# A planner's attention figures and its idle products, in a fused RWKV-5 and tanh-shrink kernel

## The chip, the cores and the metric

The kernel runs on one core of one Trainium2 chip. The metric is the device time of one execution in microseconds; shown is the median of three runs. TensorE is called PE below, VectorE DVE, ScalarE ACT, GpSimd POOL, and SyncE SP.

## The reference

Two stages follow each other. The first is a linear attention with a decaying state per head; the second is a two-layer block with the activation h - tanh(h). Cut to what matters:

```python
B, H, S, D = 4, 8, 768, 48
for t in range(S):
    cur = einsum('bhd,bhe->bhde', u * k[t], v[t])
    y[t] = einsum('bhd,bhde->bhe', r[t], state + cur)
    state = w * state + einsum('bhd,bhe->bhde', k[t], v[t])
x = y.transpose(0, 2, 1, 3).reshape(B * S, H * D)      # 3072 tokens x 384
h = x @ w_in                                           # 384 -> 2048
out = (h - tanh(h)) @ w_out                            # 2048 -> 384
```

## The kernel before

**Attention.** The sequence is cut into chunks of 64 steps. A unit is one chunk of two batch rows, so there are 24 units; unit n has the half n % 2 of the batch rows and the chunk n // 2. Its work runs through four engines in this order. SP loads r, k and v (`rt`, `kt`, `vt`; L750, three units' buffers each). DVE scales k for the state (`kw`, L894). PE turns r and `kw` with the identity into PSUM ("turn", eight products each, L763). ACT copies the turned k (`kT`, L776) and DVE scales the turned r (`rT`, L767). PE multiplies the state by `rT` ("from_state", 16 products) and `kT` by `rT` ("levels", 16 products). DVE has formed r times k and its sum (`rk` L780 and L909, `du` L784), from which ACT writes the diagonals (`at`, L788); DVE then copies the masked levels over them (`at`, L919). PE multiplies `at` by v ("outputs") and v by `kw` (the new state). ACT copies the outputs out (`xt` and `rest`, L855), DVE adds the state (L882) and decays it (L928), and POOL moves the part called `rest` into place with six small DMAs (L876). All of this PE work has the line of one helper (L717) in the profile, apart from the turns. The PSUM tile `yk_ps` holds both outputs and new state, so from_state of the next unit waits until ACT and DVE have emptied it.

**Dense part.** Two units, or 256 tokens, make one of the 12 groups j. A hidden tile is one group and two blocks of 128 hidden columns: six products h (L168, two halves of three), five ACT steps (`s`, `th`, `tg`, `q`, `small`), four DVE steps (`g` L192, `c1` L194, `c2` L196, and the masked copy over `g` at L198), and four products o (L206). Later tiles take seven half-width products of sums in place of eight (L257), for which POOL forms the sums (L242 to L246) and DVE the mixed weights (L266). The weights come as 64-bit words and are converted by DVE and ACT (L137 to L143) in 16 pieces. Passes over the first six groups take 4, 4 and 8 of the 16 hidden blocks, so that a pass needs only the pieces that are already converted.

**Order.** Nothing of this order is written by hand. Each step is a task with an engine, a cost in us, its predecessors, and a number of PE instructions (`steps`). The planner `Plan` runs forward through the tasks as the engines would, picks on each engine the ready task that is due first, and searches at random from a fixed seed for due times that end earlier. The program is then written engine by engine in that order, so any figure of a cost can move tasks on every engine. The planner also follows PE's instruction fetch: each 256 steps it works out when the next block has come, and makes PE wait if that is late.

**Idle products.** Up to the first o, the planner puts products of the identity with itself (L655) into the gaps of its plan on PE. They write a PSUM tile that nobody reads. A wide one has 512 columns and the planner's cost 0.9, a narrow one 256 columns and 0.46. `filled` counts how many fit between PE's last task and the next one:

```python
        for cost, run in filling[2]:
            n = max(0, int((start - free) / (cost * (2 if start < self.WARM else 1))))
            free += n * cost
            runs += [run] * n
        return runs
```

Of the kernel before, what the change touches and what calls it, by code (L numbers as in the profile page):

```python
# [300 lines left out]
class Plan:  # L301
# [15 lines left out]
    def add(self, engine, cost, run, after=(), due=1e9, data=0, gated=False, steps=0):  # L317
        t = SimpleNamespace(engine=engine, cost=cost, run=run, after=[x for x in after if x], due=due, data=data,
                            gated=gated, steps=steps, then=[], n=len(self.tasks))
        for x in t.after:  # L320
            x.then.append(t)
        self.tasks.append(t)
        return t
# [12 lines left out]
    def forward(self, due, until=1e9):  # L336

        ready = [max(self.FIRST, due[t.n] - self.EARLY) if t.gated else 0.0 for t in self.tasks]
        count = [len(t.after) for t in self.tasks]
        waiting = self.queues(ready, count)  # L340
        free, lanes, channel = dict(self.BEGIN), {}, 0.0
        step, bound, comes, fills = 0, self.CHUNK_0, 0.0, iter(self.fills)
        filling = next(fills, None)
        starts, done, last, first, changed = [None] * len(ready), [], 0.0, {}, set(waiting)
        self.fitted, work = [], {}
        while len(done) < len(ready):
            for e in changed:
                ts = waiting[e]
                first.pop(e, None)
                if not ts:  # L350
                    continue
                start = max(free.get(e, 0.0), min(ready[x.n] for x in ts))
                t = min((x for x in ts if ready[x.n] <= start + 1e-9), key=lambda x: (due[x.n], x.n))
                if t.data:
                    start = max(start, lanes.setdefault(e, [0.0] * self.LANES)[0])
                else:

                    soon = [x for x in ts if ready[x.n] < start + t.cost and due[x.n] < due[t.n] - self.SPARE]
                    if soon:
                        t = min(soon, key=lambda x: (ready[x.n], x.n))  # L360
                        start = max(start, ready[t.n])
                first[e] = start, t
            e = min(first, key=lambda x: (first[x][0], x))
            start, t = first[e]
            if start > until:
                break
            waiting[e].remove(t)
            changed = {e}
            end = start + t.cost
            work[e] = work.get(e, 0.0) + t.cost  # L370
            if e == "PE":
                if filling:
                    runs = self.filled(filling, free[e], start, starts)
                    self.fitted.append((free[e], t.n, runs))
                    step += 4 * len(runs)
                    if t is filling[1]:
                        filling = next(fills, None)
                step += t.steps
                if step >= bound:
                    each = t.cost / max(t.steps, 1)  # L380
                    crossed = end - (step - bound) * each
                    late = max(0.0, comes - crossed)
                    end += late
                    comes = max(crossed + late + self.ASKED * each + .3, channel) + self.COMES
                    bound += self.CHUNK
            free[e] = end
            if t.data:
                channel = max(channel, start + 1.2) + t.data
                end = max(end + self.LANDS, channel + self.LANDED) + self.slow(start)
                lanes[e] = lanes[e][1:] + [end]  # L390
            starts[t.n] = start
            last = max(last, end)
            done.append(t)
            for x in t.then:
                ready[x.n] = max(ready[x.n], end + self.hop(t, x))
                count[x.n] -= 1
                if not count[x.n]:
                    waiting[x.engine].append(x)
                    changed.add(x.engine)
        if len(done) < len(ready):  # L400
            last = until - work["PE"] - self.AHEAD * (work["DVE"] + work["ACT"])
        return last, starts, done
# [5 lines left out]
    def filled(self, filling, free, start, starts):  # L408

        for x in filling[0]:  # L410
            if starts[x.n] is None:
                return []
            free = max(free, starts[x.n] + x.cost + self.HOP)
        runs = []
        for cost, run in filling[2]:
            n = max(0, int((start - free) / (cost * (2 if start < self.WARM else 1))))
            free += n * cost
            runs += [run] * n
        return runs

    def backward(self, plan):

# [93 lines left out]
def near(ctx, tc, r, k, v, w, u, out, shared, moe_w_in, moe_w_out):  # L516
# [21 lines left out]
    add = plan.add  # L538
# [114 lines left out]
    def fills(to):  # L653
        def run(n):
# [6 lines left out]
    now = [add(e, 1.25 if e == "ACT" else .87, lambda e=e, at=at, x=x: e_of[e].dma_start(out=rows[at : at + NP, :, :D], in_=x.rearrange("(p i) d -> p i d", i=2)), due=-1, data=.05)  # L661
           for e, at, x in (("SP", 0, w), ("ACT", NP, u))]
# [3 lines left out]
    now = add("DVE", .45, lambda: V.tensor_scalar(  # L666
        by[:, :, 1:], wcol[:, :, None].to_broadcast([128, NP, SHORT]), W_LOW, W_HIGH, ALU.max, ALU.min), [cols])
    now = add("DVE", .7, lambda: V.tensor_tensor_scan(
        power.rearrange(flat), by.rearrange(flat), plus.rearrange(flat), 0.0, ALU.mult, ALU.add), [now])

    ups = add("ACT", .6, lambda: A.copy(w_up, power[:, :, None, :SHORT].to_broadcast([128, NP, 2, SHORT])), [now])
    now = add("DVE", 1.75, lambda: V.reciprocal(inverse, power), [now])
    inverted = now
    doubled = add("ACT", .6, lambda: A.copy(twice, inverse[:, :, None, 1:].to_broadcast([128, NP, 2, SHORT])), [now])
    now = tabled = add("PE", .7, table, [doubled], steps=8)
# [3 lines left out]
    now = add("POOL", 1.0, bounds, [keeps])  # L679
    now = add("PE", .2, lambda: T.matmul(tab[0:1, 0:1], ok[:, 0, :1], shared["one"], start=True, stop=True), [now, downs])  # L680
# [8 lines left out]
    def steps(generator):  # L689

        made = []

        def step():
            if not made:
                made.append(generator())
            next(made[0])

        return step

    loads, converted = [], []  # L700
    for n in range(weights.count):
# [7 lines left out]
        step = steps(lambda n=n: weights.convert(n))  # L709
        now = of + ([converted[n - 2]] if n >= 2 else [])  # L710
        for name, cost in (("DVE", .47), ("DVE", .47), ("ACT", .84), ("ACT", .84), ("DVE", .87), ("DVE", .87), ("DVE", .87)):
            now = [add(name, cost, step, now)]
# [8 lines left out]
    def unit(n):  # L721
# [3 lines left out]
        ch, half = divmod(n, 2)  # L725
        j, slot = divmod(n, L)
        steps_at = slice(ch * SHORT, (ch + 1) * SHORT)
        t = SimpleNamespace(at=ats[n % 2])
        rt, vt, kw, state = rts[n % (AHEAD + 1)], vts[n % (AHEAD + 1)], kws[n % 2], states[half]
        two = n >= L * (FIRST + 2)  # L730
# [5 lines left out]
        b1, b2, b3 = (units[n - i] if n >= i else none for i in (1, 2, 3))  # L736
        x = SimpleNamespace(rest=None, rk=None, du=None, own=None)
        units.append(x)
        product = n < OWN
        swap = n >= SWAP  # L740


        direct = j == 0
# [143 lines left out]
        more = ch < d.S // SHORT - 1  # L887

        free = [b1.cp, b1.diag] if n > 2 else [units[0].cp, units[0].diag] if n == 2 else []
        if two:  # L890
            free = [b1.xt, b1.rest, b1.add, b1.cp, b1.diag]
        turns, turned = .46, 16
        x.turn = add("PE", turns, lambda: turn(rt, r_ps), [x.r] + free, steps=turned)
        x.kw = add("DVE", .47, lambda: V.tensor_tensor(kw[:, :, :D], t.kt[:, :, :D], w_down, ALU.mult), [x.k, downs, b2.out])  # L894
        x.turn_k = x.rk = add("PE", turns, lambda: turn(t.kt if direct else kw, k_ps), [x.k if direct else x.kw] + free, steps=turned)
        both = [x.turn, x.turn_k]
# [6 lines left out]
        if product:  # L903
            now = add("ACT", 1.05, own_k, [x.kT, w_us])
            x.own = add("PE", .7, own_levels, [now, x.rT, b2.out], steps=64)
            x.diag = add("DVE", .64, lambda: V.copy_predicated(t.at, same.bitcast(I32)[:, None, None, :].to_broadcast([128, 2, NP, SHORT]), own_lev), [x.own, b2.out])
        else:
            x.rk = add("DVE", .47, own, [x.r, x.k, b2.du, b1.rk if not b1.own else None])
            now = add("DVE", .47, lambda: V.tensor_tensor(t.rk, t.rk, ub, ALU.mult), [x.rk, bonus])  # L909
            x.du = add("DVE", .47, own_sum, [now, b2.diag])  # L910
            now = add("ACT", 1.0, lambda: diagonal(range(0, H // 2)), [x.du, b2.out])
            x.diag = add("ACT", 1.0, lambda: diagonal(range(H // 2, H)), [now])
        begun = []
        if two:
            now = add("PE", .66, from_state, both + [x.rT, b1.xt, b1.rest, b1.add, b2.decay, x.kT], steps=64)
            begun = [add("ACT", .15, between, [now])]
        x.lev = add("PE", .7 if two else (1.33 if swap else 1.73) if ch else .7, levels,
                    begun + [x.kT, x.rT, b2.out] + ([b2.decay, b1.xt, b1.rest, b1.add] if ch else []), steps=128 if ch and not two else 64)
        x.cp = add("DVE", .64, lambda: V.copy_predicated(t.at, before, lev), [x.lev, b2.out] + ([] if product else [x.diag]))  # L919
        x.out = now = add("PE", .95 if direct else 1.21, outputs,  # L920
                          [x.cp, x.diag, x.v, b1.xt, b1.rest, b1.add] + ([x.extra] if direct else [x.kw]), steps=96 if direct else 128)
        if direct:
            now = x.out = add("PE", .55, to_state, [now, x.kw], steps=64)
        x.xt = add("ACT", .96 if swap else .4, to_xt, [now, last_h.get(j - FIRST - 2) if slot == 0 else None])
        if not direct:
            x.rest = add("ACT", .62 if swap else .26, to_rest, [x.xt] + (filled.get((j - 2, "all"), []) if slot == 0 else []))
# [98 lines left out]
    now, done = 22.0, 0  # L1025
# [335 lines left out]
```

## Time and profile before

| What | Value |
|---|---|
| three runs | 608.08, 605.59, 604.61 us; median 605.59 |
| profiled execution | 607.26 us, of which the span is 605.5 |
| mean TensorE clock in it | 0.989 |
| busy: PE, DVE, ACT, POOL | 582.4, 466.4, 403.3, 201.0 us |
| idle products (L655), wide | 12, of two records each; h tile's: mean 788 ns a record, x tile's: 610 |
| idle products (L655), narrow | 6 (12 records) |

The times of the profile are in microseconds from the first instruction. A product has two records (1152 for the 576 products of h), a turn's product one. The records of a group overlap (h: mean 385 ns, the next one starts some 215 ns later), so its busy time is less than count times mean. "Idle before" is the time in which an engine had nothing running ahead of an instruction, with what released it.

### The profile page before, as it was taken

How to read it: one execution, taken by the hardware profiler on the slowest of the kernel's cores; microseconds unless marked ns; L12 is line 12 of the kernel's file. 1: busy time of each engine (PE TensorE's matmuls, PEld its weight loads, DVE VectorE, ACT ScalarE, POOL GpSimd, SP SyncE). 2: the span in 40 equal slices, each digit the busy share in tenths (PEclk: the TensorE clock that was granted, in tenths of full speed). 3: DMA queues.
4: the chain of work that ended last, by engine and by line, in shares of the span. 5: the costliest groups of instructions: out<-in, count | busy, mean ns of one | idle time of the engine just before them, and what ended most of it. 6: DMA issues, size and time to landing. Idle time of an engine off the chain costs nothing.

```text
span 605.5 us, 14670 instructions
## 1 busy us (share of the span) xinstructions
PE 582.4 (96%) x5781; PEld 485.7 (80%) x5781; DVE 466.4 (77%) x782; ACT 403.3 (67%) x902; POOL 201.0 (33%) x366
## 2 busy tenths in 40 slices
PE   8877999999999999999999999999999999999996
PEld 4555767667777669999999999888889889889995
DVE  6699699999999999867677776767765775555666
ACT  3677699899866676655556686465866676565652
POOL 5002212021000123544455473425334435334540
PEclk9889899999999999999999999999999999999999
DMA  6966585967300210110111020122201100100101
GB/s 125 228 126 126 113 194 99 143 167 124 105 14 0 48 28 14 26 27 1 28 27 26 2 60 1 41 41 48 53 16 34 41 2 8 29 2 8 26 3 30
DMA packets 86326, 33.78 MB, mean 56 GB/s; under 512 B 78536, under 2 KB 80680, under 8 KB 86248
## 3 DMA queue, kind: packets, MB, share of 16 engines
q1 hardware_dynamic: 81084, 25.57, 21.1%
q0 software_dynamic: 4992, 6.99, 5.5%
q8 instruction: 47, 0.77, 0.5%
q14 instruction: 31, 0.25, 0.2%
q10 hardware_dynamic: 172, 0.20, 0.1%
HBM read 26.94 MB, written 4.72 MB: 52 GB/s over the span
## 4 chain that ended last, share of the span: by engine, by line
PE 76%; DVE 6%; DMA 5%; ACT 4%; issue 4%; SPq 3%; POOL 1%; DVEq 0%; ACTq 0%; POOLq 0%
PE h L168 37%; PE p L257 26%; PE o L206 6%; PE yk_ps L717 4%; SPq L750 3%; DMA st<-in_moe_w_in_dram 2%; DMA xt<-rest 1%; PE yk_ps L763 1%; POOL xt L876 1%; DMA st<-in_moe_w_out_dram 1%; DVE rT L767 1%; DVE at L919 1%; ACT s L177 1%; DVE tg L194 1%; DVE g L198 1%
## 5 line engine op out<-in xcount | busy, mean ns | idle before, releaser
L168 PE MATMUL h<-xt,w_in_sb 128*128 128x256 f32 x1152 | 285.7, 385 | 2.7 <-DMA xt<-rest 2.7
L168 PEld LDWEIGHTS h<-xt,w_in_sb 128*128 128x128 f32 x1152 | 214.6, 192 | 35.9 <-issue 2.1
L242 POOL TENSOR_TENSOR sg<-g 128x256 f32<-128x256 f32 x69 | 52.1, 755 | 176.7 <-DVE g L198 152.2
L257 PE MATMUL p<-mixed,sg 128*128 128x192 f32 x426 | 104.1, 326 | 0.0
L192 DVE TENSOR_TENSOR g<-h,th 128x512 f32<-128x512 f32 x96 | 65.8, 686 | 48.9 <-ACT s L177 23.0
L194 DVE SCALAR_TENSOR_TENSOR tg<-s,tg 128x512 f32<-128x512 f32 x96 | 71.1, 741 | 36.6 <-ACT tg L181 20.0
L181 ACT ACTIVATE tg<-h 128x512 f32<-128x512 f32 x96 | 57.2, 596 | 58.5 <-PE h L168 56.9
L179 ACT ACTIVATE th<-h 128x512 f32<-128x512 f32 x96 | 57.4, 598 | 39.1 <-PE h L168 39.0
L177 ACT ACTIVATE s<-h 128x512 f32<-128x512 f32 x96 | 57.4, 598 | 37.3 <-PE h L168 37.2
L876 POOL DMA_DIRECT2D xt<-rest x66 | 32.5, 499 | 146.3 <-ACT rest L855 145.8
L257 PEld LDWEIGHTS p<-mixed,sg 128*128 128x128 f32 x426 | 75.0, 190 | 0.3 <-issue 0.3
L198 DVE COPY_PREDICATED g<-small,tg 128x512 f32<-128x512 int32 x96 | 71.1, 741 | 4.7 <-DVE tg L196 0.5
L257 PE MATMUL p<-w_out_sb,g 128*128 128x192 f32 x284 | 71.9, 335 | 1.1 <-DVE at L919 1.1
L196 DVE SCALAR_TENSOR_TENSOR tg<-q,tg 128x512 f32<-128x512 f32 x96 | 67.5, 703 | 6.4 <-ACT q L183 2.4
L206 PE MATMUL o<-w_out_sb,g 128*128 128x384 f32 x192 | 71.3, 495 | 0.1
L183 ACT ACTIVATE q<-s,m1b 128x512 f32<-128x512 f32 x96 | 69.8, 727 | 0.6
L185 ACT ACTIVATE small<-s,smallb 128x512 f32<-128x512 f32 x96 | 69.6, 725 | 0.3
L257 PEld LDWEIGHTS p<-w_out_sb,g 128*128 128x128 f32 x284 | 51.8, 190 | 9.0 <-DVE at L919 1.5
L788 ACT ACTIVATE at<-same,du 128x64 f32<-128x64 f32 x184 | 47.9, 343 | 2.8 <-DVE du L784 2.6
L206 PEld LDWEIGHTS o<-w_out_sb,g 128*128 128x128 f32 x192 | 35.2, 190 | 15.8 <-DVE g L198 0.2
L246 POOL TENSOR_TENSOR sg<-sg,g 128x128 f32<-128x128 f32 x69 | 41.0, 594 | 5.1
L244 POOL TENSOR_TENSOR sg<-sg,g 128x128 f32<-128x128 f32 x69 | 36.6, 530 | 5.2
(133 smaller groups left out, 672.3 us busy)
## 6 DMA issues: line engine op xcount, KB each, us to landing
st<-in_moe_w_out_dram SPq DMA_DIRECT2D x8, 768.0 KB, 4.5
rt<-in_r_dram SPq DMA_DIRECT2D x48, 96.0 KB, 2.9
vt<-in_v_dram SPq DMA_DIRECT2D x48, 96.0 KB, 3.4
st<-in_moe_w_in_dram SPq DMA_DIRECT2D x16, 288.0 KB, 5.5
kt<-in_k_dram SPq DMA_DIRECT2D x44, 96.0 KB, 3.1
out_dram<-o POOLq DMA_DIRECT2D x44, 96.0 KB, 2.2
st<-in_moe_w_in_dram POOLq DMA_DIRECT2D x16, 96.0 KB, 6.0
xt<-rest POOLq DMA_DIRECT2D x66, 16.0 KB, 2.1
```

The source lines that it names most:

```text
L168: self.nc.tensor.matmul(t.h2[:, z], self.w_in_sb[:, t.f // 2, kk, z * 128 : (z + 1) * 128], self.xts[t.j][:, kk].rearrange("p b t -> p (b ...
L177: A.activation(out, t.h, AF.Square)
L179: A.activation(out, t.h, AF.Tanh)
L181: A.activation(out, t.h, AF.Tanh, scale=G1)
L183: A.activation(out, t.s, AF.Square, bias=self.m1b)
L185: A.activation(out, t.s, AF.Relu, bias=self.smallb, scale=-1.0)
L192: V.tensor_tensor(t.g, t.h, t.th, ALU.subtract)
L194: V.scalar_tensor_tensor(t.tg, t.s, C4, t.tg, ALU.mult, ALU.mult)
L196: V.scalar_tensor_tensor(t.tg, t.q, K1, t.tg, ALU.add, ALU.mult)
L198: V.copy_predicated(t.g, t.small.bitcast(I32), t.tg)
L206: self.nc.tensor.matmul(self.outs[i], t.g2[:, z, i * C : (i + 1) * C], self.w_out_sb[:, t.f + z, :], start=t.first and z == 0, stop=t.last ...
L257: self.nc.tensor.matmul(ps[bank][:, half * n : (half + 1) * n], a, b, start=t.first and half == 0, stop=t.last, skip_group_check=True)
```

## The change

The diff has two parts. In the planner, `filled` returns a second list: one more narrow product where at least 0.15 of a gap is left after the products that fit. And where PE's planned wait for an instruction fetch was longer than 1 us, a task that starts within 1.2 us after it gets one narrow product, if none fitted. These added ones are not counted as steps of the fetch. In the unit's tasks six figures change: a turn counts 8 PE steps instead of 16, and from_state, levels, outputs and the new state cost a little more.

```diff
@@ forward @@
-                    runs = self.filled(filling, free[e], start, starts)
-                    self.fitted.append((free[e], t.n, runs))
+                    runs, more = self.filled(filling, free[e], start, starts)
+                    if start < fetched + 1.2 and not runs:
+                        more = [filling[2][-1][1]]
+                    self.fitted.append((free[e], t.n, runs + more))
                     step += 4 * len(runs)
...
                     late = max(0.0, comes - crossed)
                     end += late
+                    fetched = end if late > 1 else fetched
@@ filled @@
-        return runs
+
+        return runs, [run] * (start - free >= .15 and start > self.WARM)
@@ unit @@
-        turns, turned = .46, 16
+        turns, turned = .46, 8
...
-            now = add("PE", .66, from_state, both + [x.rT, b1.xt, b1.rest, b1.add, b2.decay, x.kT], steps=64)
+            now = add("PE", .68, from_state, both + [x.rT, b1.xt, b1.rest, b1.add, b2.decay, x.kT], steps=64)
...
-        x.lev = add("PE", .7 if two else (1.33 if swap else 1.73) if ch else .7, levels,
+        x.lev = add("PE", .7 if two else (1.35 if swap else 1.75) if ch else .7, levels,
...
-        x.out = now = add("PE", .95 if direct else 1.21, outputs,
+        x.out = now = add("PE", .95 if direct else 1.3, outputs,
...
-            now = x.out = add("PE", .55, to_state, [now, x.kw], steps=64)
+            now = x.out = add("PE", .6, to_state, [now, x.kw], steps=64)
```

The computation is the same. In the program, the orders of all five engines differ, PE's first, from about 5 us on; on PE the last sixty microseconds are the same in both. The changed order has 11 wide and 19 narrow idle products where there were 12 and 6. Besides these twelve, no instruction is added or removed.

## The prediction

> **What bounds the kernel now.** I read the busy tenths first, then busy time in stretches of 15 us, then TensorE's waits and its timeline up to 70 us, last the order of instructions of both kernels.
>
> From the page:
>
> ```profile
> PE 582.4 (96%) x5781; PEld 485.7 (80%) x5781; DVE 466.4 (77%) x782; ACT 403.3 (67%) x902; POOL 201.0 (33%) x366
> PE   8877999999999999999999999999999999999996
> PEclk9889899999999999999999999999999999999999
> q8 instruction: 47, 0.77, 0.5%
> ```
>
> TensorE (PE) is the bound, and all that it loses lies in the first quarter. In the stretches (columns: length, then busy us of PE, PEld, DVE, ACT, POOL, then PE's clock):
>
> ```profile
> 15.00:30.00 15.00, 12.04 (x213) 8.00 (x214) 10.31 (x18) 9.00 (x29) 0.57 (x1) 0.89 1.05 230
> 30.00:45.00 15.00, 11.92 (x167) 7.90 (x168) 14.18 (x24) 11.93 (x30) 0.00 (x0) 0.89 0.67 123
> 45.00:60.00 15.00, 10.90 (x262) 7.22 (x265) 14.21 (x25) 11.52 (x39) 3.94 (x8) 0.98 0.70 127
> 60.00:75.00 15.00, 14.70 (x294) 10.75 (x286) 10.34 (x19) 10.04 (x32) 4.28 (x8) 0.79 0.54 112
> 135.00:150.00 15.00, 15.00 (x68) 11.42 (x68) 14.75 (x25) 13.80 (x29) 2.06 (x4) 1.00 0.78 133
> ```
>
> From 135 us on PE has no gap but 1.12 us at 227. Before that it idles 17.1 us, and stands at clock 0.50 from 21.9 to 25.3, 38.9 to 42.4 and 59.4 to 66.2 us: 6.8 us of speed lost. DVE is nearly full from 30 to 60 us and from 90 us. PE's waits (us in total, times, longest):
>
> ```profile
> PE yk_ps L717 <- DVE at L919: 3.8, 5, 1.8
> PE x_ps L763 <- DVE kw L894: 3.1, 1, 3.1
> PE h L168 <- DMA xt<-rest: 2.7, 2, 1.5
> PE yk_ps L717 <- DVE state L882: 2.2, 3, 1.1
> ```
>
> They are the attention chain: turn, scale (`rT`), from_state, levels, `at` (L919), outputs. In the timeline (start, length):
>
> ```profile
> 29.89 4.56 PE L655 MATMUL x_ps<-ident 128*128 128x512 f32 x10
> 34.38 0.66 PE L717 MATMUL yk_ps<-at,vt 64*48 64x64 f32 x32
> ...
> 38.87 0.66 PE L763 MATMUL x_ps<-ident,kw 64*128 64x64 f32 x8 [3.08 <-DVE kw L894]
> 39.46 4.27 PE L168 MATMUL h<-xt,w_in_sb 128*128 128x256 f32 x12
> ```
>
> Idle products (L655) run to 34.4, though `at` was written at 31.3; then PE waits for `kw`, falls to half clock and needs 4.27 us for a tile's h that later takes 2.6.
>
> **What the Trainium skill says.** "TensorE: Matmul & The Clock Gate", Part 1, What's actually happening: the clock halves after an idle window of some 3.4 us and returns after a busy one, on a free-running grid. The trace agrees on the length (3.4, 3.4, 6.8 us). It doesn't need a wholly idle window: those ahead of the drops held 1.2 to 1.6 busy us, while ones with 2.2 kept the clock. The same page, Architectural detail: VectorE and ScalarE take instructions strictly in order. It agrees: `at` of unit 1 ran at 20.66 behind a conversion (L137) that had waited 2.91 us for its DMA. "Runtime: NRT & Kernel Launch", Instruction fetch mechanics: fetches come in blocks of 256 instructions, mostly hidden. Queue 8 shows 47 packets of 16 KB; one fetch-like stall stands out (0.72, "issue", at 18.1).
>
> **The change part by part.** PE's useful work U is the same in both. Per product, start to start: h 0.43, o 0.65, the seven 0.32; a turn 0.40; from_state, levels, outputs, state 0.48, 0.58, 0.48, 0.47. Thus the time changes by idling, half clock and idle products alone, and at any place I compare D = (time after - time before) - (U after - U before). DVE's times I get from sums of its row means in the order, times 0.87: from `rT` of unit 3 to that of unit 4 the rows give 8.98 and the trace 7.64, to unit 5 9.07 and 8.08.
>
> *Idle products.* The order has 13 more narrow ones (two records of 0.215: 0.43 us) and one wide one less (0.90): 12 more, seven at the ends of gaps, five by the fetch rule. PE is lengthened by 13 x 0.43 - 0.90 = 4.7 us, all before the first o. Lower bound of their cost: 0, where PE idled (12.9 us up to 60), or less than 0 through the clock; upper bound 4.7. Below they are counted where they stand.
>
> *Order, steps 1 to 7.*
> 1. To 17 us only three narrow ones come in; the waits there (0.39, 0.71) hide most: +0.2.
> 2. `at` of unit 1 now precedes the conversion: 18.6, not 20.66. But three wide products (2.7) stand ahead of its outputs: 21.2 instead of 21.4. The window to 21.9 is full, so the first half-clock stretch goes. On SP's queue a half of `vt` passes the first weight pair: 0.6 us later landing of that pair (19.7 to 20.3).
> 3. `kw` of unit 2 passes L142 and L143 (24.0, not 25.3). from_state 2: 27.6 against 28.83, with tile 0's h (2.6) now behind it: D = +1.4.
> 4. That h stands where the five wide ones stood; outputs 2 at 32.8 against 34.38. `kw` of unit 3 has 1.95 less of rows ahead (-1.7 us). The wait of 3.08 and the second half-clock stretch go. from_state 3: 40.5 against 43.66, same U: D = -3.2.
> 5. Given back: o of tile 0 needs L198, whose row sum is 38.65 against 38.06; about 47.6 in both. from_state 4: 49.5 against 50.7, 1.3 less U: D = 0.
> 6. `rest` of group 1 is ready 3 us earlier, so its six DMAs (POOL's queue, still ahead of the next weight pair) land before 56, and the waits 1.55 and 1.19 go. from_state 5 waits for DVE instead (rows 49.3 against 50.3): 58.5 against 59.44, U +1.3: D = -2.2.
> 7. Without the third half-clock stretch (3.4) units follow each 6.7 us of PE work, not 8. from_state 8: 84.3 against 87.47, U +1.3: -4.5. from_state 11: 105.8 against 114.50, U -2.6: -6.1. DVE allows it, since conversions are put off: rows ahead of that point 99.0 against 106.7.
>
> *After that* before still loses 0.27, 1.14 (unit 12) and 1.12 (first of the seven, on `at` of unit 15). After has 22 us of PE work between unit 12's turn and from_state, and two o and an h more between unit 15's levels and its outputs: -2.5. From there only places of units move, the last 60 us on PE not at all: 0, covered by PE's backlog. SP's loads and POOL's `rest` move by a few places; their cover is the three-unit load buffers and, late, idle DMA.
>
> Chain sum: -8.6. Off it: half clock near 57 us, where PE now idles 1.2 to 2.4 us (half a chance of 1.7): 0.9; waits in units 5 to 10, whose cover after the last outputs is mostly 3.4 us (before, that cover cost 0, 0.30 and 0.81): 1.2; units 16, 17 and 22 with 1.0 to 1.3 between turn and from_state (1.3 cost 1.14 at unit 12, 0 at unit 19): 0.9; overrun of idle products: 0.6. **-5.0 us.** The profiled execution took 607.26 (605.5 span, 1.8 around it): 602.3. It lies 1.7 above the median; from the median, 605.59 - 5.0 = 600.6.
>
> **Rivals.**
> - *DVE and the clock keep the bound.* Row sums ahead of from_state 6 and 7 are 1.0 and 1.8 larger than before; if PE goes cold there for two windows (3.4) the gain of step 7 goes: about -1.5, 604.1. For: DVE was full from 30 to 60. Against: the first of the seven needs the same DVE rows (232.1, before 231.8), but after has 6.4 more U behind it there.
> - *Idle products on the path: slower.* PE takes them in order; where the planner's gap doesn't exist they push turn, outputs and from_state of units 0 to 4. If the order wins nothing and 3.5 of the 4.7 us are uncovered: 609.1; it decides from 3.0 uncovered. For: five wide ones held outputs 2 back by 3.1 us. Against: PE idled 12.9 us up to 60.
> - *The fetch rule misses.* A turn is now counted as 8 instructions, yet the trace shows 8 products and 8 weight loads. Then five narrow ones (2.2 us) fill nothing, and the rest wins little: about 605 to 608.
>
> **How the numbers follow.** Forecast 0.62 (faster 0.57, same 0.05), DVE and clock 0.20 (0.07, 0.13), idle products 0.12 (same 0.01, slower 0.11), fetch 0.06 (same 0.03, slower 0.03). "Same" is within 0.5%, 3.0 us, about what a measurement of this kernel tells from none. Together faster 0.64, same 0.22, slower 0.14. The range runs from the chain sum (-8.4, 597.2) past the second case to +1.4 (607.0), leaving out most of the slower cases and a little below.
>
> **What would show it.** Right: PE's clock 1.00 from 18 to 42 us; no wait for `kw` near 36; from_state 5 before 59.4 with two tiles of h following; idle of PE up to 135 us under 12 us; no wait at the first of the seven. Wrong: a clock of 0.50 longer than one window, outputs starting late behind L655 with `at` long written, or new waits over 1 us at units 16 to 23.

## The result and the profile after

The changed kernel takes **603.25 us** (median of 17 executions, 600.95 to 608.05) against 606.21 us of the kernel before (17 on the same chip, 602.16 to 609.25). The ratio is 0.9951, with a 95% interval of 0.9933 to 0.9968. That is half a per cent faster, about the least that can be told from no change. It lies inside the forecast range, 2.65 us above the forecast of 600.6. The profiled execution of after took 601.34 us (span 599.6), that of before 607.26. Lines behind the planner stand four further down in after: L655 is now L659, L717 L721, L763 L767, L894 L898, L919 L923.

From the page of after, the lines that answer to those shown of before:

```profile
PE 582.5 (97%) x5805; PEld 485.9 (81%) x5805; DVE 466.9 (78%) x782; ACT 403.6 (67%) x902; POOL 203.6 (34%) x366
PE   8999999999999989999999999999999999999996
PEclk9999999999999999999999999999999999999999
q8 instruction: 47, 0.77, 0.5%
```

The clock row has no 8 left. In stretches of 15 us (length, then busy us of PE, PEld, DVE, ACT and POOL, then PE's clock, the DMA share and GB/s):

```profile
15.00:30.00 15.00, 14.16 (x223) 8.69 (x224) 11.15 (x20) 10.73 (x32) 0.27 (x1) 1.00 1.13 230
30.00:45.00 15.00, 13.80 (x258) 10.07 (x257) 14.97 (x26) 13.74 (x37) 0.00 (x0) 1.00 0.71 126
45.00:60.00 15.00, 13.63 (x286) 9.78 (x287) 14.76 (x27) 12.46 (x37) 4.29 (x8) 1.00 0.73 143
60.00:75.00 15.00, 13.70 (x290) 8.73 (x279) 14.00 (x27) 12.04 (x39) 3.97 (x8) 1.00 0.92 147
```

PE is busy 2 to 3 us more in each stretch from 15 to 60 us, at full clock. Its waits (us in total, times, longest):

```profile
PE yk_ps L721 <- DVE state L886: 2.2, 3, 0.9
PE yk_ps L721 <- issue: 1.7, 2, 1.1
...
PE x_ps L767 <- DVE at L923: 1.2, 1, 1.2
PE h L168 <- DMA xt<-rest: 1.0, 2, 0.6
```

The wait for `kw` (3.1) is gone, and that of outputs for `at` (3.8) is down to 0.5. "Issue", in which PE waits for nothing that the profile shows, has grown from 0.7 to 1.7. The timeline says where (start, length, idle before in brackets):

```profile
31.73 0.67 PE L721 MATMUL yk_ps<-at,vt 64*48 64x64 f32 x32 [0.28 <-ACT st L140]
32.19 0.39 PE L721 MATMUL yk_ps<-vt,kw 64*48 64x48 f32 x12
33.15 0.47 PE L721 MATMUL yk_ps<-vt,kw 64*48 64x48 f32 x20 [0.57 <-issue]
33.55 0.46 PE L767 MATMUL x_ps<-ident,rt 64*128 64x64 f32 x8
34.35 2.83 PE L168 MATMUL h<-xt,w_in_sb 128*128 128x256 f32 x12 [0.34 <-DVE w_in_sb L143]
37.11 0.46 PE L767 MATMUL x_ps<-ident,kw 64*128 64x64 f32 x8
...
75.39 0.60 PE L721 MATMUL yk_ps<-at,vt 64*48 64x64 f32 x28 [1.09 <-issue]
```

`kw` of unit 3 is turned at 37.11, at once, where before waited until 38.87, and a tile of h stands ahead of it. The "issue" gaps split groups of 32 records, that is 16 small products (12 + 20; 2 + 28 and two more).

**The sum.** Span = PE's idle time (the gaps) + idle products + useful work, which is all else that PE is busy with. Before: 605.5 = 23.0 + 17.9 + 564.6. After: 599.6 = 17.1 + 23.4 + 559.1. Gaps and idle products only changed places (40.9 and 40.5). The useful instructions are the same in both; that they took 5.5 us less is the half clock, of which before had 13.7 us (3.4, 3.4 and 6.8) and after none ahead of its last two microseconds. In before 12.2 us of useful work lie in those stretches; at half speed that costs 6.1 us, near the 5.5.

### The profile page after: what moved, and what is told of

Same layout as the page of the kernel before. It is cut to its first block, busy times and chain, and to the rows that moved or that the text cites. A ratio compares the mean times of both kernels' runs of the same rounds, so it can differ in the third digit from the quotient of the medians.

```text
span 599.6 us, 14682 instructions
## 1 busy us (share of the span) xinstructions
PE 582.5 (97%) x5805; PEld 485.9 (81%) x5805; DVE 466.9 (78%) x782; ACT 403.6 (67%) x902; POOL 203.6 (34%) x366
## 3 DMA queue, kind: packets, MB, share of 16 engines
q1 hardware_dynamic: 81084, 25.57, 21.8%
## 4 chain that ended last, share of the span: by engine, by line
PE 70%; DVE 12%; ACT 6%; SPq 4%; DMA 3%; issue 3%; POOL 0%; DVEq 0%; ACTq 0%; POOLq 0%
PE h L168 34%; PE p L257 25%; PE o L206 5%; PE yk_ps L721 4%; SPq L754 3%; DMA xt<-rest 1%; ACT at L792 1%; DMA kt<-in_k_dram 1%; DVE g L198 1%; DVE tg L194 1%; DVE tg L196 1%; DVE g L192 1%; SPq L123 1%; PE yk_ps L767 1%; DVE mixed L266 1%
## 5 line engine op out<-in xcount | busy, mean ns | idle before, releaser
L194 DVE SCALAR_TENSOR_TENSOR tg<-s,tg 128x512 f32<-128x512 f32 x96 | 68.7, 716 | 52.9 <-ACT tg L181 28.1
L179 ACT ACTIVATE th<-h 128x512 f32<-128x512 f32 x96 | 57.4, 597 | 33.4 <-PE h L168 33.2
L198 DVE COPY_PREDICATED g<-small,tg 128x512 f32<-128x512 int32 x96 | 75.3, 784 | 4.4 <-DVE tg L196 0.5
L244 POOL TENSOR_TENSOR sg<-sg,g 128x128 f32<-128x128 f32 x69 | 43.2, 626 | 5.0
L246 POOL TENSOR_TENSOR sg<-sg,g 128x128 f32<-128x128 f32 x69 | 36.9, 535 | 5.1
```

What stands on the lines that cost most here:

```text
L179: A.activation(out, t.h, AF.Tanh)
L194: V.scalar_tensor_tensor(t.tg, t.s, C4, t.tg, ALU.mult, ALU.mult)
L198: V.copy_predicated(t.g, t.small.bitcast(I32), t.tg)
```

## The experiments

Two theories. **Order**: the gain is in the places of the attention chain and the dense tiles, above all `kw` of unit 3, and any other order can have it or lose it. **Figures and products**: the figures of the change are nearer to the chip, or the idle products keep the clock. Each ratio is against before on the same chip; it is not the quotient of the medians shown.

### The change again

The same program, in a second series.

> The changed kernel once more, so that the three others of this series stand beside it on one chip. Order theory and clock theory alike: some 0.5% under before, 603 us, with scatter that follows the mean clock (0.999 near 601.5, 0.994 near 606.5).

Measured: 602.92 us (16 executions), ratio 0.9944 [0.9922, 0.9967], the same as the first time. Its profiled execution took 604.03. Timeline:

```profile
74.69 0.31 PE L721 MATMUL yk_ps<-at,vt 64*48 64x64 f32 x2
76.83 0.60 PE L721 MATMUL yk_ps<-at,vt 64*48 64x64 f32 x28 [1.83 <-issue]
...
77.77 2.69 PE L168 MATMUL h<-xt,w_in_sb 128*128 128x256 f32 x6
```

The "issue" gap is at the same instruction as in the first profile, 1.83 long instead of 1.09, and here PE falls to half clock behind it: six records of h take 2.69, not 1.56. The two series together show how much that matters: 19 executions with a mean clock of 0.998 or more have a median of 602.2 us, 8 with 0.995 to 0.997 have 603.9, and 6 with 0.993 or 0.994 have 607.4. Before depends on its clock too. Its median clock is 0.988; of its 62 executions in the last series four reached 0.997, and these took 603.1 to 603.7 us. At equal clock, then, before is no slower than the change: what parts their medians goes together with the clock.

### The order without the added products

```diff
-                    self.fitted.append((free[e], t.n, runs + more))
+                    self.fitted.append((free[e], t.n, runs))
```

> The changed order on all engines, without the 12 added narrow products (11 wide and 7 narrow idle products stay). Order theory: the gain is the order's, so this is within 1 us of the changed kernel, about 603, and its profile has a gap in place of each product left out (some 5 us more idle time up to 55 us, same start of from_state 5 near 55.6). Clock theory: the added products are what holds the clock, so it falls to 0.50 at least once before 45 us in the profile, and the time is 605 to 606. Slower-product theory: 4.7 us less work on PE ahead of the chain, so it is 1 us or more faster than the changed kernel.

Measured: 604.51 us (11), ratio 0.9955 [0.9938, 0.9972]. The order alone gives the gain, or most of it. Without the added products the median is 1.6 us higher than in the change, but the intervals overlap. The profile is not as the order theory had it: the clock fell to 0.50 from 26.2 to 29.6 and from 46.7 to 50.1 us, the sign that the clock theory named, and from_state 5 began at 57.0, not near 55.6. The time, 604.5, lies between the numbers of these two theories. So the added products do hold the clock up (median 0.998 with them, 0.993 without); what that is worth is at most the 1.6 us.

### The added products on the order before

The two rules for more narrow products, with all six figures as before. Against the change:

```diff
-        turns, turned = .46, 8
+        turns, turned = .46, 16
...
```

> The order of before on all engines, with only the two rules for added narrow products. Order theory: no change from before, within 1 us, and the wait for kw near 36 us stays. Clock theory: 2 to 3 us faster than before, since the half-clock stretches from 21.9 and 38.9 us go. Product theory: slower by up to 2 us, the products standing ahead of turns that are already late.

Measured: 607.19 us (22), ratio 1.0007 [0.9990, 1.0024]: nothing. Its profiled execution was its slowest, 612.32, with "issue" gaps of 3.82 at 21.8 us and 2.29 at 119.8, and 17 us of half clock ahead of its end. More products in the gaps did not keep the clock in it. Over all executions the median clock is 0.991 against before's 0.988, without a gain in time.

### No idle products at all, on both orders

```diff
-                    self.fitted.append((free[e], t.n, runs + more))
+                    self.fitted.append((free[e], t.n, []))
```

After's order without its 30 products:

> The changed order with none of its 30 idle products, so PE stands idle in their places (18 us less of PE's busy time). Order theory: the chain's dates hold, but PE is cold in most of the first 45 us: turns, levels, outputs and the first h take twice their time, 3 to 6 us slower than the changed kernel, 606 to 609. If idle products mostly stand in the way: 603 or less.

Before's order without its 18:

> Before's order and figures with no idle products at all, 18 fewer. The change's order without any gave 603.5 us, as with all 30. Theory P (idle products are worth their place only where they keep the clock, and on before's order they keep it in no window that matters while they hold outputs back, as the five wide ones did): the time falls, 602 to 605 us, and hardly scatters. Theory K (they keep the clock, and without them before loses more than they cost): slower, 608 to 613 us. Theory N (products and gaps only change places): 605.5 to 607.5 us, as before.

Measured: 603.53 us (6 executions, 603.02 to 603.73), ratio 0.9939 [0.9922, 0.9957]; and 606.77 us (22), ratio 0.9995 [0.9979, 1.0011]. (The diff is that of after; before has `runs` alone in the line.) The first is neither the 606 to 609 of the order theory nor the 603 or less of its rival; the second is theory N's number. On neither order do all the idle products together move the median by more than 0.6 us. And the orders keep their distance of 3.2 us without a single one. Waits of PE in the first, after's order:

```profile
PE yk_ps L721 <- DVE at L923: 3.9, 3, 2.0
...
PE yk_ps L721 <- DVE rT L771: 3.4, 2, 1.8
...
PE x_ps L767 <- DVE kw L898: 1.6, 1, 1.6
```

and in the second, before's order:

```profile
PE yk_ps L717 <- DVE at L919: 6.8, 6, 2.7
PE x_ps L763 <- DVE kw L894: 6.2, 1, 6.2
```

With nothing to fill it, the wait for `kw` of unit 3 stands bare in before's order: 6.2 us in one piece, from 34.7 to 40.8. After's order has 1.6 (unit 2). PE idles 30.6 us in the first profile and 34.2 in the second, and useful work takes 571.2 and 570.6. Both show some 10 us of half clock after 30 us. Ahead of that, to 31.5 and 30.4 us, the trace has no record of the clock, so that the mean clock counts this time as full; but in both the small products run at about half speed there (32 records of from_state at 27.9 us of the first take 1.10, later 0.66). So the clock is not what parts these two. And the idle products do keep PE at full speed in the first 30 us, but that was worth nothing on the median.

### Half clock at 59 us filled, on the order before

```diff
+            if hasattr(self, "spare") and t.j == 1 and t.f == 0 and z == 0:
+                for _ in range((0, 7, 5)[kk]):
+                    self.nc.tensor.matmul(self.spare()[:, 384:], self.ident, self.ident, start=True, stop=True, skip_group_check=True)
...
```

The added products share a PSUM bank with running sums of o, which lose part of their value by it; no instruction of before is left out.

> Before's order and figures, and 12 products of the identity with 128 columns written where nobody reads: 7 ahead of the second and 5 ahead of the third h product of tile 2, that is in the two gaps at 55.4 to 57.0 and 57.7 to 58.8 us of the profile of before. They leave those gaps' waits as they are (the transfers of `rest`) but keep PE busy in the window that ends at 59.4. Theory K (the half-clock stretch of 59.4 to 66.2 costs before its speed there, 3.4 us): no half clock from 59 to 66, and 2 to 3.4 us less, about 603.5 to 605. Theory C (the chain through DVE and the transfers sets the dates after 60, and PE would have waited for it anyway): the stretch goes but the time stays within 1.5 us of before, 605.5 to 608.

Measured: 607.17 us (22), ratio 1.0009 [0.9992, 1.0025]. The stretches of its profile, same columns as above:

```profile
45.00:60.00 15.00, 12.64 (x266) 9.70 (x266) 14.40 (x26) 11.50 (x39) 3.94 (x8) 1.00 0.76 132
60.00:75.00 15.00, 14.64 (x321) 10.77 (x320) 11.85 (x22) 11.85 (x40) 4.28 (x8) 1.00 0.69 144
```

The clock is 1.00 where before had 0.98 and 0.79, so the stretch went. The median did not move: theory C's number. The profile is not clean evidence for C, though: it has an "issue" gap of 3.20 at 20.0 where before, with the same instructions up to there, had 0.72 at 18.1. Over all 22 executions the mean clock is 0.990, before's 0.989, so the others had about as much half clock as before; where it fell in them is not on record. What the stretch at 59 us costs by itself stays open.

### One part of the figures alone

The turn's 8 steps only, and then the five costs only, both without the new product rules.

```diff
-        turns, turned = .46, 16
+        turns, turned = .46, 8
```

> Of the change only one figure is taken: a turn counts 8 steps of the fetch instead of 16; the five costs and both rules for idle products stay as before. This gives a third order of all engines. Theory A (what helps is figures that stand nearer to the chip, and a turn is 8 products in the trace): part of the gain comes with this figure alone, about 605 us, ratio 0.996 to 0.998. Theory B (any new figure only draws another order from the planner's random search, and the order of the change is a good draw): the time can fall on either side, within 600 to 612, and the profile's waits up to 60 us tell which, not the figure. Under both, a shift below zero needs from_state of unit 5 to start before 59.4 us or the half-clock stretch near 60 to go.

```diff
-            now = add("PE", .66, from_state, ...)
+            now = add("PE", .68, from_state, ...)
...
-        x.lev = add("PE", .7 if two else (1.33 if swap else 1.73) if ch else .7, levels,
+        x.lev = add("PE", .7 if two else (1.35 if swap else 1.75) if ch else .7, levels,
...
```

> Of the change only the five costs of from_state, levels, outputs and new state are taken (each 0.02 to 0.09 us longer); a turn still counts 16 steps, and no rule for idle products is added. Theory A (nearer figures help): the other part of the gain, about 605 us, ratio 0.996 to 0.998; together with the turn's figure it should make up the 0.9955 that the order without added products gave. Theory B (a draw of the search): either side, within 600 to 612, and the two parts need not add up to the whole.

Measured: 602.39 us (6), ratio 0.9916 [0.9890, 0.9941]; and 603.50 us (7), ratio 0.9931 [0.9900, 0.9962]. Each part alone gives the whole gain or more, so they do not add up, as theory A needs. The first has the lowest median of all kernels run. It beats before; against the change its interval overlaps, so that one is not settled.

### Other draws of the search

The planner's seed, 5 in all kernels above, set to 6 and 7, with the figures before and with those of the change.

```diff
-        chance = Random(5)
+        chance = Random(6)
```

Change, seed 6:

> The changed kernel, all figures and rules kept, with another seed of the planner's random search (6 instead of 5). Theory A (the figures and rules of the change make good orders): about the same time as the changed kernel, 601.5 to 604.5 us, ratio 0.990 to 0.997. Theory B (the order of the change is one draw among many): the time differs from the changed kernel's by more than 2 us, on either side, 598 to 610.

Before, seed 6, and before, seed 7:

> The kernel before, figures and rules unchanged, with another seed of the planner's random search (6 instead of 5). Theory A (the gain comes from better figures): about the time before, 604.5 to 608.5 us. Theory B (an order is one draw, and draws differ by some us whatever the figures; with the figures of the change seed 6 gave 608.2 and seed 5 gave 602.9): it differs from before by more than 2 us on either side, 600 to 611.

> As the run with seed 6, with seed 7. Theory A: 604.5 to 608.5 us. Theory B: anywhere from 600 to 611 us; the three seeds of the figures before together spread by 4 us or more. In the profile, the sum of idle and idle products of TensorE up to 60 us should order these kernels (28 to 30 us in those of 602 to 604.5, 33 in that of 608).

Change, seed 7:

> The changed kernel with seed 7. Theory A (figures and rules make good orders, and seed 6 was an exception): 601.5 to 604.5 us. Theory B (a draw): anywhere from 600 to 611 us; the mean of the changed figures over three seeds then lies within 2 us of the mean of the figures before.

Measured, in us, with the ratio to before with seed 5:

| figures | seed 5 | seed 6 | seed 7 | mean |
|---|---|---|---|---|
| before | 606.8 | 603.58, 0.9947 [0.9929, 0.9965] | 605.76, 0.9987 [0.9969, 1.0004] | 605.4 |
| change | 603.1 | 608.19, 1.0012 [0.9995, 1.0028] | 605.97, 0.9990 [0.9972, 1.0009] | 605.8 |

(Seed 5: the runs of before in the last series, and the mean of the change's two series.) Theory B holds. The figures before with seed 6 are as fast as the change; the change with seed 6 has lost its whole gain. Over three seeds the means of the two sets of figures differ by 0.4 us, which three draws that spread by 3 and 5 us cannot tell from nothing. One number missed: the spread of before's figures is 3.2 us, not the 4 expected.

Before with seed 7, the slower of the two, has the late `kw` again (waits of PE):

```profile
PE yk_ps L717 <- DVE at L919: 5.3, 4, 2.5
PE x_ps L763 <- DVE kw L894: 4.9, 1, 4.9
```

Before with seed 6, the fast one, has no wait for `kw` in its list. Why the change with seed 6 loses its gain is another thing; its timeline:

```profile
17.62 0.46 PE L721 MATMUL x_ps<-rT,kT 48*64 48x64 f32 x16
21.00 0.70 PE L721 MATMUL x_ps<-rT,kT 48*64 48x64 f32 x16 [2.92 <-issue]
21.63 3.34 PE L659 MATMUL h<-ident 128*128 128x512 f32 x4
24.90 0.58 PE L721 MATMUL yk_ps<-at,vt 64*64 64x64 f32 x24
```

Levels of unit 1 stand still for 2.92 in the middle of their 32 records. PE then takes two wide idle products at half clock (3.34), and outputs of unit 1 start at 24.90 though `at` was written at 22.6; in after they start at 20.72. From 30 to 45 us it spends 8.8 of 15 us on idle products, after 4.9. Idle products and gaps up to 60 us come to 33.4 us, in after 28.7.

### One view that orders them

Useful work of PE begun by 90 us: records of h, o, turns and attention, at the prediction's start-to-start times (estimates; all fourteen traces hold the same 5745 records of useful work). The view was picked after the runs.

| kernel | work by 90 us | its profiled time |
|---|---|---|
| change | 55.7 | 601.3 |
| before, seed 6 | 54.7 | 602.0 |
| change, no idle products | 54.7 | 603.5 |
| change, none added | 54.3 | 603.4 |
| change, again | 53.7 | 604.0 |
| turn's 8 alone | 52.4 | 603.2 |
| change, seed 6 | 51.6 | 609.3 |
| five costs alone | 51.4 | 606.1 |
| before, 59 us filled | 51.1 | 606.3 |
| change, seed 7 | 50.9 | 604.8 |
| before, seed 7 | 50.4 | 605.8 |
| before, no idle products | 49.5 | 606.5 |
| before | 49.0 | 607.3 |
| before, added products | 47.4 | 612.3 |

With exceptions of 2 to 4 us, the change with seed 6 above all, it is a falling line: what PE has behind it at 90 us, it does not have to do later. From before to the change the work rises by 6.7 and the time falls by 5.9. The expected order by idle and idle products up to 60 us did worse: change with seed 7 has 35.2 us of them, more than seed 6 with its 33.4, and is faster.

The sum says how an order wins, and it is not always the same way. Before with seed 6 has as much half clock as before (13.7 us), but its gaps and idle products come to 36.9 us, not 40.9; over all executions its median clock is no better (0.987), and it is 3.2 us faster. The change has 40.5 of them, and no half clock. The change with seed 6 has 47.0, and little half clock (6.8).

## Why the prediction was right, and where it wasn't

**The cause** was right: the order. The order alone gives 0.9955, and with no idle product in either kernel the distance is still 3.2 us. The prediction let it win through earlier dates of the attention chain, with the half clock going as gaps close. The half clock weighs more than that suggests: by the sum, 5.5 of the 5.9 us between the two profiles are half clock and 0.4 are gaps and idle products, and executions of before that kept the clock are as fast as the change. The dates by themselves are shown only in the pair without idle products, where they are 3.6 us of idle time. Whether they would be worth anything between before and the change with the clock held in both is not shown. Counting the added products where they stand, as near nothing, was right within 1.6 us.

**Step 1 and 2.** Outputs of unit 1 started at 20.72 (forecast 21.2), and the first half-clock stretch went.

**Steps 3 and 4**, `kw` and from_state: from_state 2 at 27.10 (27.6), outputs 2 at 31.73 (32.8), from_state 3 at 39.42 (40.5). The waits of 3.08 and the second half-clock stretch went. D after step 4 was -4.2, forecast -3.2. The kernels without idle products confirm this step by itself: `kw` of unit 3 costs 6.2 us in one order and nothing in the other.

**Step 5 failed: "given back; D = 0".** The o of tile 0 started at 45.81, not 47.6, and from_state 4 at 47.27, not 49.5: D = -3.44 + 1.3 = -2.1. The row sums on DVE of 38.65 and 38.06 were taken for one date, and that date from before's o, 47.80. But in before L198 had ended at 46.7, and o did not wait for it. In after L198 ended at 45.7: up to its start DVE was busy for the same time in both (34.7 and 34.8 us), but idle 1.2 us less. Rows of DVE are not its waits, and those had changed with the order.

**Steps 6 and 7** carried that error on: from_state 5 at 55.56 (58.5), 8 at 81.26 (84.3), 11 at 104.61 (105.8; D -7.3, forecast -6.1). The waits for `rest` shrank to 0.58 and 0.45. No stretch of half clock came at 59 us. Its own worth, counted into step 7, was not confirmed: filling it on before's order left the median where it was.

**After that**: before lost its 2.5 us, as said. After lost 2.9 that had no term: 0.41 at 118.5 (o, for ACT's `part`), 1.23 at 210.9 (a turn, for `at`), 0.56 at 220.4, 0.71 at 248.7. The 0.9 for units 16, 17 and 22 was not needed at all; the cover was missed elsewhere. -7.3 - 2.5 + 2.9 = -6.9; the spans differ by 5.9, and the last 1.0 is not accounted for. That the forecast of -5.0 lies so near is in part luck: the chain won 1.2 us more than forecast up to from_state 11 and lost 2.9 later without a term, and the 3.6 us set aside off the chain were meant for other places.

**The step that was mis-sized most is the one from the profile to the median.** The profiles differ by 5.9 us, the medians by 3.0. The forecast of -5.0 was subtracted from a median as if both kernels' profiled executions lay alike to their medians; before's lay 1.05 above, after's 1.9 below. The changed kernel takes some 602.2 us where the clock holds, and 604 to 608 where it does not (mean clocks of 0.997 and less). The term for the clock (half a chance of 1.7, near 57 us) had the place wrong and the size too small. In the repeated profile it came at 78 us, behind an "issue" gap that the prediction had nowhere.

**Rivals.** "Idle products on the path" did not happen in this order but does in its neighbour with seed 6, where they hold outputs of unit 1 back by 2.3 us. "The fetch rule misses" was right about the products (at most 1.6 us from all twelve) and wrong about the order, which did not need them. Of the five signs named, four came in full: clock 1.00 from 18 to 42 us, no wait for `kw`, 9.2 us of PE's idle up to 135 us, and no wait at the first of the seven. Of the fifth, from_state 5 came before 59.4, but one tile of h followed it and the other stood ahead. Of the signs against, none came.

Two figures of the prediction are off without bearing on its outcome. The windows ahead of before's three drops held 1.6, 0.3 and 1.2 busy us, so not all lie between 1.2 and 1.6. And the lower end of the range takes -8.4 for a chain sum of -8.6.

## What to carry to other kernels

When a figure of a planner's cost moves the time, run the planner with other seeds before crediting the figure: here three seeds spread by 3 us with the old figures and by 5 with the new, and the means lay 0.4 apart. Write the span as gaps, idle products and useful work, and compare executions at equal clock, before saying how an order wins. What the profile then shows (here one late `kw` on DVE, 6 us bare) might be fixed by hand or as a due time; no run here tried it. Fill work that only keeps an engine busy has to be measured against none at all; here 18 and 30 products were worth nothing on the median.

## What the runs showed of the hardware

**Late instruction fetches are not small.** "Runtime: NRT & Kernel Launch", Instruction fetch mechanics, in the Trainium skill, calls the crossing of a block "mostly hidden". Here PE stood still, with nothing that it waited for, 20 times for over 0.5 us in the fourteen profiles, mostly inside groups of small products. In seven profiles it did so at least once for over 2 us: 3.82 (before with seed 6), 3.82, 2.92, 2.82 (change with seed 7), 3.20 and 2.25 near 21 us; 2.64 and 2.44 near 98; 2.29 near 120; 2.26 near 111. The DMA records of the traces tie these gaps to fetches. Each of the 20 ends 1.3 to 1.6 us after a 16 KB packet of queue 8 has landed; of PE's 101 other waits over 0.5 us only 9 do. With 59 us filled, the packet ahead of the gap at 20.0 started at 17.0 us, in before at 15.2, with the same instructions up to there: the longer gap is a later fetch. What delayed it stays open.

```profile
20.81 0.70 PE L717 MATMUL x_ps<-rT,kT 48*64 48x64 f32 x15 [3.82 <-issue]
```

This line is from before with seed 6, the second fastest profile of all: a gap near 21 us was made up there. In the order of the change, at 75 us, the same kind of gap of 1.1 to 1.8 us has dense work queued behind it.

**A window need not be idle to cost the clock.** The clock changes of each trace lie on a grid of 3.41 us. Cut on this grid, the fourteen traces show 25 falls from full to half clock ahead of their last microseconds. The window ahead of each held 0.3 to 1.9 us of busy PE. Of the windows at full clock that held 2.0 us or more, none was followed by a fall; seven that held 1.6 to 2.0 were not either. In before, the fall at 59.4 us came with no gap longer than 1.55 us.

**Half clock is not priced by its length.** Useful work took 5.5 us more in before with 13.7 us of half clock, but 1.3 more with 3.4 (the change, again), 2.6 with 6.8 (none added), 1.4 with 6.8 (change with seed 6), 0.95 with 6.8 (change with seed 7) and 4.3 with 13.7 (before with seed 6), each against the 559.1 of the change. That is 0.1 to 0.4 us for each us of half clock, as a part of each stretch is idle or idle products. Among the 62 executions of before, a straight line through time and mean clock gives 4.5 us for each hundredth, which is 12 us of half clock, so 0.37 for each us. "TensorE: Matmul & The Clock Gate", What's actually happening, in the Trainium skill, has a free-running window for it, one that does not start afresh with the kernel. The first record of full clock agrees: it comes at 4.5 us in one profile of the change and at 6.4 in the other. So does the scatter of 601 to 608 us among executions of one program.
